# Background matmuls of an attention stream: one 128x128 matmul each in place of four 128x32 column tiles

## The chip, the cores and the metric

The kernel runs on one core of one Trainium2 chip. The metric is the device time of one execution in microseconds (us). Three runs of the kernel before took 1203.0, 1203.92 and 1205.25 us; the median is 1203.92 us.

## The reference

The computation is one transformer layer on 2048 tokens of width 1024, in bf16: layer norm, attention with 32 heads of width 32, a residual, a second layer norm, and a feed-forward block of width 3584 with tanh-GELU and another residual.

```python
x = A_x
h = x + _A_ref(_layernorm(x, axis=-1), A_wqkv, A_wo)      # softmax attention, 32 heads, then @ wo
h2 = h + _B_ref(_layernorm(h, axis=-1), B_w1, B_b1, B_w2, B_b2)   # gelu(x @ w1 + b1) @ w2 + b2
```

## The kernel before, in words

**Engines.** TensorE (PE) does all matrix products, ScalarE (ACT) does the softmax exponentials and the tanh of the GELU, VectorE (DVE) moves results out of PSUM and does the layer norms, SyncE (SP) issues the loads and stores. Each engine runs its own instruction stream in order, and semaphores tie the streams together.

**The attention stream.** The queries are cut into four chunks of 512. For each chunk and each of 16 pairs of heads, `attention_round` runs 8 times, so there are 512 rounds in all. A round issues three kinds of work.

- **qk** (`Att.qk`, L634): four matmuls with a contraction of 32 rows each. They sit in four *row* tiles of the array, at row 0, 32, 64 and 96, run side by side, and fill four PSUM banks with scores (keys on the partitions, 512 queries along the free dimension).
- **exp** (L643): two ACT instructions, each on two banks (128x1024), write the exponentials `PT` in bf16. Three pairs of banks go round, so one pair is free while two are in use.
- **pv** (`Att.pv_unit`, L654 and L658): for each exponential tile four matmuls with 32 output columns each, in four *column* tiles of the array: two heads of P times V, and two with a stationary block of ones that sum the softmax denominators. They accumulate in bank 6 over the 16 key tiles.

**The background stream.** Exponentials take long, so PE gets other work to fill the time: in the first chunk the rest of the Q, K and V projections (`proj`, `proj_v`), in the later chunks the output projection, the second layer norm and the feed-forward block of the chunk before (`wo`, `ln2`, `ffn1`, `ffn2`) and the late part of the query projection (`late_q`). It all goes through PSUM bank 7 (banks 4 and 7 in the opening). After the last attention chunk, the last chunk's `wo`, `ln2`, `ffn1` and `ffn2` run alone, with all eight banks; this is the tail.

**`mm`** issues one background product of 128 contraction rows, 128 output partitions and 512 (in `proj_v` 256) free elements. Its argument `narrow` is true in the background stream and false in the tail. With `narrow` it issues four matmuls (L439), each with 32 columns of `lhsT` as its stationary operand, at column tiles 0, 32, 64 and 96, all with the same moving operand. Without, it issues a single 128x128 matmul (L443). So in the kernel before the background and pv both use the array as four column tiles.

**What sets the order.** The kernel is first recorded as a graph of tasks, and `Graph.schedule` plays it through with estimated costs to fix the order of each engine's stream at build time. `pick_pe` takes a ready qk first, then a pv when four or five of them wait, else a background task. The task of one `mm` carries a cost `occ` and a `mode` ("col", "row" or "full"); a change of mode adds 0.1 us in this plan, and `pick_pe` looks at the mode "col" too. The plan decides the order alone; on the chip the streams run as fast as their semaphores let them. The planner's marks for a narrow `mm` are one task of mode "col".

**Transposes.** `transposes` (L508) are 128x128 matmuls in the background stream before and after the change; eight of them form one tile.

Of the kernel before, what the change touches and what calls it, by code (L numbers as in the profile page):

```python
# [284 lines left out]
def build_kernel(nc, A_x, A_wqkv, A_wo, B_w1, B_b1, B_w2, B_b2, out):  # L285
# [123 lines left out]
    psum = nc.alloc_psum_tensor("ps", [P, 8, 512], F32)  # L409
    B_ps = [gr.buf() for _ in range(8)]  # L410
# [18 lines left out]
    def pe(fns, occ, reads=(), writes=(), kind="bg", mode="full", prio=0, after=()):  # L429
        return gr.add(E.PE, fns, occ, 0.16, reads, writes, prio, kind, mode, after)  # L430

    def mm(bank, lhsT, rhs, start, stop, reads, narrow, cols=(0, 512)):

        c0, c1 = cols
        occ = MM * (c1 - c0) / 512.0 + 0.003
        if narrow:
            fns = []
            for j in range(4):
                fns.append(lambda p, j=j: p.matmul(psum[32 * j:32 * j + 32, bank, c0:c1], lhsT[:, 32 * j:32 * j + 32], rhs,  # L439
                                                   start=start, stop=stop, tile_position=(0, 32 * j), skip_group_check=True))  # L440
            pe(fns, occ, reads=reads, writes=[B_ps[bank]], mode="col")
        else:
            pe(lambda p: p.matmul(psum[:, bank, c0:c1], lhsT, rhs, start=start, stop=stop),  # L443
               occ, reads=reads, writes=[B_ps[bank]], mode="full")

    def act(fn, n, reads=(), writes=(), prio=0, ap_bias=False, kind=""):
        return gr.add(E.Activation, fn, c_act(n, ap_bias), 0.14, reads, writes, prio, kind)
# [7 lines left out]
    def dma(out_ap, in_ap, nbytes, reads=(), writes=(), prio=0, noncontig=False, after=()):  # L455
        def fn(s):
# [10 lines left out]
         reads=[B_ident], writes=[B_ident])  # L467
# [67 lines left out]
    def proj(which, g, tc, bank, evac, direct=False):  # L535

        blk, c = divmod(which * D + g * P, 512)
        for dc in range(DC):
            mm(bank, Wall[:, blk, dc, c:c + P], xnT[:, tc, dc, :], dc == 0, dc == DC - 1,
               [B_W[blk][c // P]] + B_xnTt[tc], True)  # L540
        s = cnt["sg"] % NSG
        cnt["sg"] += 1
        if evac == "act":
            act(lambda a: a.activation(stg[:, s, :], psum[:, bank, :], ACT.Copy), 512,
                reads=[B_ps[bank]], writes=[B_stg[s]], prio=-1)
        else:
            dve(lambda v: v.tensor_copy(stg[:, s, :], psum[:, bank, :]), c_dve_ps(512), reads=[B_ps[bank]], writes=[B_stg[s]])  # L547
        if which == 1:
            for pr in range(2):
                for half in range(2):  # L550
                    dve(lambda v, pr=pr, half=half: v.tensor_copy(
                        KT2[64 * half:64 * half + 64, 2 * g + pr, tc, :, :],
                        stg[64 * pr:64 * pr + 64, s, 256 * half:256 * half + 256]), c_dve(256, 4),
                        reads=[B_stg[s]], writes=[B_KT[4 * (2 * g + pr) + tc][half]])
        else:
            if direct:
                for pr in range(2):
                    for half in range(2):
                        dve(lambda v, pr=pr, half=half: v.tensor_copy(
                            QT2[64 * half:64 * half + 64, g, pr, :], stg[64 * pr:64 * pr + 64, s, :]), c_dve(512, 4),  # L560
                            reads=[B_stg[s]], writes=[B_QTh[g][half][pr]], prio=-1)
            else:
                dma(qd[g, tc], stg[:, s, :], P * 1024, reads=[B_stg[s]], writes=[B_qd[g][tc]], prio=0)
# [12 lines left out]
    def late_q(R, qc, gs):  # L576

        dma(R.xq[:, :, :], xd[qc - 1], P * 8192, reads=[B_xd[qc - 1]], writes=[R.B_xq], prio=0)
        for g2 in range(gs // 2, G // 2):
            s = wblock(R, A_wqkv[:, 256 * g2:256 * g2 + 256], 0)  # L580
            for k in range(2):
                g = 2 * g2 + k
                for dc in range(DC):
                    mm(7, R.w1[:, s, dc, k * P:k * P + P], R.xq[:, dc, :], dc == 0, dc == DC - 1,
                       [R.B_w1[s], R.B_xq], True)
                o = R.next("os", R.nos)
                dve(lambda v, o=o: v.tensor_copy(R.ost[:, o, :], psum[:, 7, :]), c_dve_ps(512),
                    reads=[B_ps[7]], writes=[R.B_ost[o]])
                dma(qd[g, qc], R.ost[:, o, :], P * 1024, reads=[R.B_ost[o]], writes=[B_qd[g][qc]], prio=0)

    def proj_v(tt, q, bank, evac):

        blk, c = divmod(256 * q, 512)
        blk += 4
        for k in range(2):
            tc, t4 = divmod(tt + k, 4)
            for dc in range(DC):
                mm(bank, xnT[:, tc, dc, t4 * P:(t4 + 1) * P], Wall[:, blk, dc, c:c + 256], dc == 0, dc == DC - 1,
                   B_W[blk][c // P:c // P + 2] + [B_xnTt[tc][t4]], True, cols=(256 * k, 256 * k + 256))
        dst = V[:, tt:tt + 2, 256 * q:256 * q + 256]  # L600
        src = psum[:, bank, :].rearrange("p (t c) -> p t c", t=2)
        wr = [B_V[4 * (tt + k) + q] for k in range(2)]
        if evac == "act":
            act(lambda a: a.activation(dst, src, ACT.Copy), 512, reads=[B_ps[bank]], writes=wr, prio=-1)
        else:
            dve(lambda v: v.tensor_copy(dst, src), c_dve_ps(512), reads=[B_ps[bank]], writes=wr)  # L606
# [190 lines left out]
    for k in range(80):  # L797
        pe(lambda p: p.matmul(psum[:, 6, 0:256], ident[:, :], b2t[:, 0:256], start=True, stop=True), 0.12,  # L798
           reads=[B_ident, B_b2t], writes=[B_ps[6]], kind="warm")
# [207 lines left out]
```

## Time and profile before

| what | value |
|---|---|
| median of three runs | 1203.92 us (1203.0 to 1205.25) |
| span of the profiled execution | 1417.9 us |
| mean granted TensorE clock in it | 0.749 of full speed |
| PE busy | 1366.2 us, 96% of the span, 17326 matmuls |
| ACT busy | 1085.3 us, 77% |
| DVE busy | 673.2 us, 47% |
| last exponential starts | 1253.9 us after the span's start |

The profile shows a single execution, and the profiler gives no other time for it than its span, 1417.9 us, from the first instruction to the last. That is 214 us above the median of the three timed runs, which carry no profile. A matmul's end is modelled in these records, and its start is observed, so in what follows matmuls are judged by the distance from one start to the next. A *group* is what one call issues together: four tiles that start within some 12 ns of each other, or one full matmul. The granted clock is what a throttle lets through to TensorE.

### The profile page before, as it was taken

To read this page: it belongs to the slowest core of one execution; us is meant where nothing else is said; L and a number is where in the kernel's file an instruction comes from. 1 tells how busy PE (TensorE), PEld (TensorE's weight loads), DVE (VectorE), ACT (ScalarE), POOL (GpSimd) and SP (SyncE) were. 2 spreads that over 40 slices of the span, in tenths; PEclk is the share of its full clock that TensorE was granted. 3 is DMA by queue.
4 is the path that set the end of the run, shared out by engine and by line. 5 is a ranking of instruction groups with operands and counts; after the bars stand their busy time and mean duration, and the time that the engine had idled before them with its cause. 6 is when DMAs were issued, how large, how long until landed. Compare 5 with 4: busy or idle time off the path is not lost.

```text
span 1417.9 us, 37847 instructions
## 1 busy us (share of the span) xinstructions
PE 1366.2 (96%) x17326; PEld 510.9 (36%) x17336; DVE 673.2 (47%) x1165; ACT 1085.3 (77%) x1189; POOL 37.9 (3%) x96
## 2 busy tenths in 40 slices
PE   8999999999999999999999999999999999978999
PEld 5544443433333333332333333333333333324333
DVE  7354444443546774223547762225677612245710
ACT  4778787878888888888888888888988888844500
POOL 2000000000100000000100000000000000001000
PEclk7777777777777777777777777777777777766777
DMA  6800000025343222303342230422323322202222
GB/s 165 224 2 13 28 13 14 13 72 156 101 122 101 76 69 72 124 16 98 107 124 71 83 98 16 124 71 63 107 73 98 102 66 85 87 0 75 74 93 71
DMA packets 165793, 112.29 MB, mean 79 GB/s; under 512 B 25345, under 2 KB 162817, under 8 KB 164866
## 3 DMA queue, kind: packets, MB, share of 16 engines
q1 hardware_dynamic: 165634, 109.87, 26.2%
q8 instruction: 136, 2.23, 0.7%
q14 instruction: 23, 0.19, 0.1%
HBM read 98.58 MB, written 11.27 MB: 77 GB/s over the span
## 4 chain that ended last, share of the span: by engine, by line
PE 91%; ACT 4%; DVE 3%; issue 1%; POOL 1%; DMA 0%; POOLq 0%; DVEq 0%
PE ps L439 48%; PE ps L654 17%; PE ps L634 12%; PE ps L443 10%; ACT PT L643 3%; PE ps L658 2%; PE ps L798 1%; ACT xnT L512 1%; DVE a_xh L748 1%; PE ps L508 1%; DVE V L606 0%; DVE stg L547 0%; DVE Osb L668 0%; DVE Dsb L666 0%; DMA a_w1r<-in_A_wqkv_dram 0%
## 5 line engine op out<-in xcount | busy, mean ns | idle before, releaser
L643 ACT ACTIVATE PT<-ps 128x1024 bf16<-128x1024 f32 x1024 | 989.2, 1025 | 180.5 <-PE ps L634 166.1
L654 PE MATMUL ps<-PT,V 128*32 128x512 bf16 x2048 | 383.4, 457 | 13.7 <-DVE V L606 6.2
L658 PE MATMUL ps<-PT,ones 128*32 128x512 bf16 x2048 | 384.8, 458 | 0.0
L439 PE MATMUL ps<-a_w2r,gT 128*32 128x512 bf16 x2688 | 241.9, 452 | 0.0
L634 PE MATMUL ps<-QT,KT 32*128 32x512 bf16 x2048 | 216.7, 414 | 7.4 <-ACT PT L643 7.3
L439 PE MATMUL ps<-a_hnT,a_w1r 128*32 128x512 bf16 x2688 | 215.2, 454 | 4.0 <-DVE a_xh L748 3.2
L654 PEld LDWEIGHTS ps<-PT,V 128*32 128x32 bf16 x2048 | 103.3, 104 | 143.9 <-issue 89.3
L634 PEld LDWEIGHTS ps<-QT,KT 32*128 32x128 bf16 x2048 | 51.5, 91 | 272.3 <-ACT PT L643 164.5
L439 PE MATMUL ps<-xnT,Wall 128*32 128x512 bf16 x1344 | 111.6, 453 | 7.0 <-ACT xnT L512 4.8
L439 PEld LDWEIGHTS ps<-a_w2r,gT 128*32 128x32 bf16 x2688 | 77.3, 109 | 112.0 <-issue 103.3
L673 DVE RECIPROCAL Dsb<-Dsb 128x128 f32<-128x128 f32 x128 | 115.1, 928 | 1.0
L439 PEld LDWEIGHTS ps<-a_hnT,a_w1r 128*32 128x32 bf16 x2688 | 70.6, 107 | 108.0 <-issue 71.4
L782 DVE SCALAR_TENSOR_TENSOR a_ost<-ps,hch 128x512 bf16<-128x512 f32 x24 | 16.6, 692 | 189.8 <-PE ps L439 189.7
L658 PEld LDWEIGHTS ps<-PT,ones 128*32 128x32 bf16 x2048 | 103.5, 104 | 6.6 <-issue 6.6
L748 DVE TENSOR_SCALAR a_xh<-ps,b1f 128x512 bf16<-128x512 f32 x84 | 63.1, 751 | 81.3 <-PE ps L439 80.2
L666 DVE COPY Dsb<-ps 64x512 f32<-64x512 f32 x64 | 44.4, 694 | 101.5 <-PE ps L658 100.1
L439 PE MATMUL ps<-Wall,xnT 128*32 128x256 bf16 x2048 | 83.8, 314 | 0.0
L547 DVE CAST stg<-ps 128x512 bf16<-128x512 f32 x40 | 27.5, 689 | 89.2 <-PE ps L439 89.2
L443 PE MATMUL ps<-a_hnT,b_w1r 128*128 128x512 bf16 x219 | 64.5, 470 | 2.1 <-ACT a_hnT L512 1.5
L439 PEld LDWEIGHTS ps<-Wall,xnT 128*32 128x32 bf16 x2048 | 57.6, 107 | 22.7 <-issue 11.3
L443 PE MATMUL ps<-a_w2r,gT 128*128 128x512 bf16 x219 | 64.1, 461 | 0.5
L439 PE MATMUL ps<-a_w1r,OT 128*32 128x512 bf16 x768 | 63.1, 453 | 0.8 <-DVE hch L719 0.5
(69 smaller groups left out, 875.5 us busy)
## 6 DMA issues: line engine op xcount, KB each, us to landing
a_w2r<-in_B_w_dram SPq DMA_DIRECT2D x56, 512.0 KB, 4.6
a_w1r<-in_B_w_dram SPq DMA_DIRECT2D x42, 512.0 KB, 3.9
a_w1r<-in_A_wo_dram SPq DMA_DIRECT2D x16, 512.0 KB, 4.7
QT<-q_scratch SPq DMA_DIRECT2D x60, 128.0 KB, 2.8
b_w1r<-in_B_w_dram SPq DMA_DIRECT2D x14, 512.0 KB, 3.8
a_w1r<-in_A_wqkv_dram SPq DMA_DIRECT2D x11, 512.0 KB, 5.1
xrb<-in_A_x_dram SPq DMA_DIRECT2D x16, 256.0 KB, 3.9
Wall<-in_A_wqkv_dram SPq DMA_DIRECT2D x16, 256.0 KB, 5.4
```

The source lines that it names most:

```text
L439: fns.append(lambda p, j=j: p.matmul(psum[32 * j:32 * j + 32, bank, c0:c1], lhsT[:, 32 * j:32 * j + 32], rhs, start=start, stop=stop, tile ...
L443: pe(lambda p: p.matmul(psum[:, bank, c0:c1], lhsT, rhs, start=start, stop=stop), occ, reads=reads, writes=[B_ps[bank]], mode="full")
L508: pe(lambda p, dc=dc: p.transpose(psb[:, bank, dc * P:(dc + 1) * P], src_ap[:, dc * P:(dc + 1) * P], ident[:]), 0.064, reads=[B_src, B_ide ...
L547: dve(lambda v: v.tensor_copy(stg[:, s, :], psum[:, bank, :]), c_dve_ps(512), reads=[B_ps[bank]], writes=[B_stg[s]])
L634: return p.matmul(psum[:, 2 * u + j, :], KT2[r0:r0 + 32, p16, tc, i, :], QT2[r0:r0 + 32, qs, pr, :], start=True, stop=True, tile_position= ...
L643: act(lambda a, u=u, s=s: a.activation(PT[:, s, :, :], psum[:, 2 * u:2 * u + 2, :], ACT.Exp, bias=0.0, scale=SCALE), 1024, reads=[B_ps[2 * ...
L654: fns.append(lambda p, j=j, h=h: p.matmul(psum[32 * j:32 * j + 32, bank, :], V[:, kt, 32 * h:32 * h + 32], PT[:, s, j, :], start=first, st ...
L658: fns.append(lambda p, j=j: p.matmul(psum[64 + 32 * j:96 + 32 * j, bank, :], ones32[:, :], PT[:, s, j, :], start=first, stop=last, tile_po ...
L666: dve(lambda v: v.tensor_copy(Dsb[64 * pr:64 * pr + 64, :], psum[64:128, bank, :]), c_dve_ps(512), reads=[B_ps[bank]], writes=B_Dsb[pr], p ...
L673: dve(lambda v, k=k: v.reciprocal(Dsb[:, 128 * k:128 * k + 128], Dsb[:, 128 * k:128 * k + 128]), 0.93, reads=[B_Dsb[0][k], B_Dsb[1][k]], w ...
L748: dve(lambda v, i=i, fc=fc, bank=bank: v.tensor_scalar(R.xh[:, i, :], psum[:, bank, :], b1f[:, fc:fc + 1], None, ALU.add), c_dve_ps(512), ...
L782: dve(lambda v, o=o, t4=t4, j=j, bank=bank: v.scalar_tensor_tensor(R.ost[:, o, :], psum[:, bank, :], 0.5, hch[:, t4, 512 * j:512 * j + 512 ...
```

## The change

`mm` issues one 128x128 matmul in every case. Its stationary operand is the whole 128x128 `lhsT`, the moving operand and the PSUM region stay as they were. The planner's marks are kept: the task still has the same cost and, for `narrow`, the mode "col".

```diff
         occ = MM * (c1 - c0) / 512.0 + 0.003
-        if narrow:
-            fns = []
-            for j in range(4):
-                fns.append(lambda p, j=j: p.matmul(psum[32 * j:32 * j + 32, bank, c0:c1], lhsT[:, 32 * j:32 * j + 32], rhs,
-                                                   start=start, stop=stop, tile_position=(0, 32 * j), skip_group_check=True))
-            pe(fns, occ, reads=reads, writes=[B_ps[bank]], mode="col")
-        else:
-            pe(lambda p: p.matmul(psum[:, bank, c0:c1], lhsT, rhs, start=start, stop=stop),
-               occ, reads=reads, writes=[B_ps[bank]], mode="full")
+        pe(lambda p: p.matmul(psum[:, bank, c0:c1], lhsT, rhs, start=start, stop=stop),
+           occ, reads=reads, writes=[B_ps[bank]], mode="col" if narrow else "full")
```

The built programs have the same order on every engine; on PE each four instructions of L439 become one. 10336 column-tile matmuls become 2584 full ones (2072 with 512 free elements, 512 with 256). Matmuls of the tail, qk, pv and the transposes are untouched.

## Prediction

> **What bounds the kernel now.** I read the page from the top: busy shares, the clock by slices, the chain that ended last.
>
> ```profile
> span 1417.9 us, 37847 instructions
> ...
> PE 1366.2 (96%) x17326; PEld 510.9 (36%) x17336; DVE 673.2 (47%) x1165; ACT 1085.3 (77%) x1189; POOL 37.9 (3%) x96
> ...
> PEclk7777777777777777777777777777777777766777
> ...
> PE 91%; ACT 4%; DVE 3%; issue 1%; POOL 1%; DMA 0%; POOLq 0%; DVEq 0%
> ```
>
> PE is busy nearly throughout, holds 91% of the chain, and gets a clock of 0.75. So the profiled execution is bound by PE. The groups show who could be next:
>
> ```profile
> L643 ACT ACTIVATE PT<-ps 128x1024 bf16<-128x1024 f32 x1024 | 989.2, 1025 | 180.5 <-PE ps L634 166.1
> ...
> L634 PE MATMUL ps<-QT,KT 32*128 32x512 bf16 x2048 | 216.7, 414 | 7.4 <-ACT PT L643 7.3
> ```
>
> ACT's exponentials wait 166 us for qk; qk waits 7 us for them. Wherever PE is longer, ACT is later.
>
> The timed runs are 214 us shorter, so their balance must be worked out. The program has 4384 groups of 512 columns (2072 + 256 background, counting two of 256 as one; 512 qk, 1024 pv, 520 tail) and some 104 equivalents in warm-up and transposes. In the tail's run of full matmuls the starts lie 292 ns apart at clock 0.752 (504 pairs), in column-tile runs 277 ns (2544 pairs); at full clock that is about 216 ns. 4488 x 0.216 = 969 us of pure streaming, or 1289 us at 0.752. The runs take 1204, so their clock is higher: at least 969/1204 = 0.80, and with 1069 mode changes at some 0.08 us and 40 us of opening and tail waits about 0.90. ACT's floor in the attention part is 992 exponentials at 0.912 us (starts back to back lie 0.904 to 0.920 apart) plus 84 tanh at 0.52 = 948 us; PE's there, at full clock, is 969 - 49 (the opening: 152 groups and 72 equivalents) - 114 (the tail: 520 and 8) + 90 (changes of mode) = 896. So between clock 0.90 and 1.0 PE and ACT are within 6% of each other, and PE has at most 52 us to spare.
>
> **What the change does.** The order of the streams stays. *Removed:* three of four instructions of each background group. That pays only if the group is held by something other than its 512 columns. The 256-column groups answer this: with the same eight instructions (four weight loads, four matmuls) they follow each other in 138 ns on average (430 pairs), which is 256 columns at 0.75. So issue keeps up at 17 ns an instruction, and a 512 group would need no more than 138 of its 277. I book no gain. Weight loads are hidden in both shapes:
>
> ```profile
> L439 PEld LDWEIGHTS ps<-a_hnT,a_w1r 128*32 128x32 bf16 x2688 | 70.6, 107 | 108.0 <-issue 71.4 <-DVE a_xh L748 23.9
> ...
> L443 PEld LDWEIGHTS ps<-a_hnT,b_w1r 128*128 128x128 bf16 x224 | 25.6, 115 | 40.6 <-issue 39.2 <-ACT a_hnT L512 1.4
> ```
>
> 107 and 115 ns lie inside a pitch of 277 to 292. The Trainium skill (TensorE: Matmul & The Clock Gate, Weight-path perf modes) says a full 128-column bf16 weight gets a fast load, and TensorEngine Tiling (Array Packing), Restrictions, that column tiling disables it: a rule in favour of the change. The two rows differ by 8 ns the other way; with a hidden load the sum by the rule stays the same.
>
> *Added:* changes of the array's division. Before, background and pv are both column tiles and follow each other at the common pitch; only qk (row tiles) stands between:
>
> ```profile
> 468.22 0.40 PE L634 MATMUL ps<-QT,KT 32*128 32x512 bf16 x4
> 468.63 2.10 PE L439 MATMUL ps<-a_hnT,a_w1r 128*32 128x512 bf16 x28
> 470.66 0.42 PE L634 MATMUL ps<-QT,KT 32*128 32x512 bf16 x4
> 471.02 0.45 PE L439 MATMUL ps<-a_hnT,a_w1r 128*32 128x512 bf16 x4
> 471.24 0.48 PE L654 MATMUL ps<-PT,V 128*32 128x512 bf16 x2
> ```
>
> Columns: start, length, engine, line, operation. Row to column costs 0.41 and 0.36 us instead of one pitch; background to pv costs 0.22, nothing extra. Over the trace: column to row 406 ns (449 pairs), row to column 354 (491). After the change each border of background and pv is a border of full and column. In the built order the changes of mode go from 1069 to 1813: 372 pairs (full to column and back) are new, and some 370 qk neighbours turn from column to full. The trace of before has this very sequence near the end, where the tail's `wo` begins inside the last rounds:
>
> ```profile
> 1234.45 0.43 PE L654 MATMUL ps<-PT,V 128*32 128x512 bf16 x2
> 1234.46 0.49 PE L658 MATMUL ps<-PT,ones 128*32 128x512 bf16 x2
> 1234.88 0.97 PE L443 MATMUL ps<-a_w1r,OT 128*128 128x512 bf16 x3
> 1235.78 0.45 PE L634 MATMUL ps<-QT,KT 32*128 32x512 bf16 x4
> 1236.16 1.24 PE L443 MATMUL ps<-a_w1r,OT 128*128 128x512 bf16 x4
> 1237.33 0.41 PE L654 MATMUL ps<-PT,V 128*32 128x512 bf16 x2
> ```
>
> pv to full took 0.43 here; the trace has 426, 385, 382 and one 579 that held a wait, mean of the three 398 ns. Full to pv took 360, 380, 360, mean 367. From transposes to pv it is 171 against 70 between transposes (17 and 226 pairs), again +100.
>
> - **Term 1, new changes.** Against a pitch of 284 (between 277 and 292): (398 - 284) + (367 - 284) = 197 ns a pair, x 372 = 73 us. Bounds: 158 ns (fastest of each, against 292) gives 59; 256 ns (579 kept in, against 277) gives 95.
> - **Term 2, qk beside full.** qk to full 379 (one) and to transposes 367 (6) against 354; full to qk 415 (one) against 406. 370 x (13 + 3 to 9), about 6 us; bounds 0 and 12.
> - **Term 3, catching up.** In column runs the first pitch after a change is 248 ns (476 runs), 32 below the 280 or so of the later ones: part of the stop is regained. 744 more runs, x 32 = -24 us. This may belong to the throttle, whose pitches jump between 266 and 318; and a run of a single group has no second pitch. Bounds -24 and 0; I take -24.
> - **Term 4, pitch in runs.** 277 against 292 is the same first-pitch effect, since column runs are short and the tail's long; taken as 0. No bound beyond Term 3.
>
> Sum: 73 + 6 - 24 = 55 us on PE, between 59 + 0 - 24 = 35 and 95 + 12 = 107. In the profile's own time nothing covers this, as PE is the chain: 1418 + 55 = **1473 us**. In the timed runs the clock is 0.90 or more; a stop counted in cycles shrinks to 0.8 of itself (58 of the 73), but so does the regained part, and a stop made of latencies keeps its size. I keep 55: 1204 + 55 = **1259 us**.
>
> The skill has the rule against this change (TensorEngine Tiling, Tiling Modes, Key Properties): a change of tiling mode drains TensorE, while another tile of one mode does not. It names no price; TensorE: Matmul & The Clock Gate gives a drain of about 128 cycles, an estimate of 53 ns at 2.4 GHz and 40 us for 744, against 55 by the rows.
>
> No DMA, wait or buffer is added. pv and qk come later by the stops in front of them; waiting on them are the exponentials on ACT, then the next qk.
>
> **The rivals.**
>
> - *ACT covers it.* If the timed clock is 1.0, PE has 52 us to spare in the attention part and the 55 are mostly hidden: about 1204 + 8 = 1212. For it: 948 against 896. Against: the timed attention part is then 1204 - 75 (opening, 82 less half of the 16 that the clock can give) - 124 (tail, 161 less 37 for the clock) = 1005, 57 above ACT's floor, so ACT would already be waiting for PE; and the plan fills each round of PE with background.
> - *The stops cost their upper bound* and nothing is regained: 1204 + 107 = 1311. For it: at a higher clock the throttle's catching up may go. Against: three of four samples.
> - *Faster.* At the timed clock the four-tile group may be held by issue. The most this can be is the excess of 1005 over PE's 896, 109 us over some 2200 background groups, 50 ns each. Taking it away and adding 55 leaves PE at 951 and the time at about 1150. It decides from 25 ns a group (55/2200). Against: 138 ns for eight instructions.
> - *Nothing happens:* the array passes from full to column tiles without a stop: 1204. Against: every sample.
>
> **Numbers.** Forecast 1259 (within 1230 to 1295): 0.64. Hidden by ACT, 1205 to 1230: 0.16. Upper bound, 1295 to 1320: 0.11. Faster, 1150: 0.06. Nothing, 1204: 0.03. A measurement of this kernel tells apart about 0.2%, 2.4 us. Faster 0.06; same 0.03 and 0.01 of the hidden case: 0.04; slower 0.90. The range leaves out faster, nothing and the upper bound: 1210 to 1300.
>
> **What would show it.** In the profile after: PE matmuls 17326 less some 7750; pv to background near 398 and background to pv near 367 where they were at the common pitch; runs of background unchanged at 280 to 290; ACT's wait for qk up from 166 by about 55; DVE and the tail unchanged. If pv to background stays at 280, Term 1 is wrong. If the stops show in the profile but the timed runs stay near 1210, ACT covered them. If background runs are shorter in pitch than before, issue did matter.

## Result and the profile after

| | before | after |
|---|---|---|
| median | 1203.93 us (1203.0 to 1205.25, 4 runs) | 1255.85 us (1255.47 to 1256.85, 4 runs) |
| ratio to before | | 1.0433, 95% interval 1.0418 to 1.0448 |

The change costs 51.9 us, or 4.3%. The forecast was 1259 us, within 1210 to 1300.

The profiled execution on which the prediction rests had a granted clock of 0.75 and took 1417.9 us, while all later ones had 0.99 and took what the timed runs take, so from here on before is read in a second profile of the same kernel (experiment e1, span 1200.8 us). Its page, in the rows that were shown above (the last one is the chain of work that ended last, by engine):

```profile
span 1200.8 us, 37847 instructions
...
PE 1126.8 (94%) x17326; PEld 465.6 (39%) x17336; DVE 668.4 (56%) x1165; ACT 1059.5 (88%) x1189; POOL 38.1 (3%) x96
...
PE 74%; ACT 12%; DVE 10%; DMA 2%; issue 1%; POOL 1%; SPq 0%; POOLq 0%; DVEq 0%
```

The same rows of after:

```profile
span 1253.7 us, 22353 instructions
...
PE 1192.3 (95%) x9584; PEld 421.2 (34%) x9584; DVE 670.9 (54%) x1165; ACT 1073.1 (86%) x1189; POOL 37.9 (3%) x96
...
PE 82%; DVE 8%; ACT 7%; issue 1%; DMA 1%; POOL 1%; POOLq 0%; DVEq 0%; SPq 0%
```

The records of PE hold 7742 matmuls fewer (the built programs differ by 7752), and PE is busy 65 us longer. It holds 82% of the chain in place of 74%. Where the time goes is seen in one place of the second chunk's `ffn2`, the same instructions in both. The timeline of before (e1), PE alone (columns: start, length, engine, line, operation):

```profile
505.53 0.40 PE L634 MATMUL ps<-QT,KT 32*128 32x512 bf16 x4
505.85 0.40 PE L439 MATMUL ps<-a_w2r,gT 128*32 128x512 bf16 x4
506.08 0.38 PE L654 MATMUL ps<-PT,V 128*32 128x512 bf16 x2
506.08 0.38 PE L658 MATMUL ps<-PT,ones 128*32 128x512 bf16 x2
506.29 0.39 PE L439 MATMUL ps<-a_w2r,gT 128*32 128x512 bf16 x4
506.51 0.38 PE L654 MATMUL ps<-PT,V 128*32 128x512 bf16 x2
506.52 0.38 PE L658 MATMUL ps<-PT,ones 128*32 128x512 bf16 x2
506.73 0.82 PE L439 MATMUL ps<-a_w2r,gT 128*32 128x512 bf16 x12
507.48 0.40 PE L634 MATMUL ps<-QT,KT 32*128 32x512 bf16 x4
```

And of after:

```profile
520.54 0.40 PE L627 MATMUL ps<-QT,KT 32*128 32x512 bf16 x4
520.86 0.39 PE L436 MATMUL ps<-a_w2r,gT 128*128 128x512 bf16 x1
521.18 0.39 PE L647 MATMUL ps<-PT,V 128*32 128x512 bf16 x2
521.19 0.39 PE L651 MATMUL ps<-PT,ones 128*32 128x512 bf16 x2
521.52 0.39 PE L436 MATMUL ps<-a_w2r,gT 128*128 128x512 bf16 x1
521.84 0.39 PE L647 MATMUL ps<-PT,V 128*32 128x512 bf16 x2
521.84 0.39 PE L651 MATMUL ps<-PT,ones 128*32 128x512 bf16 x2
522.17 0.82 PE L436 MATMUL ps<-a_w2r,gT 128*128 128x512 bf16 x3
522.92 0.39 PE L627 MATMUL ps<-QT,KT 32*128 32x512 bf16 x4
```

From one qk to the next it is 1.95 us before and 2.38 after. Background to pv and pv to background take 0.22 us before and 0.32 to 0.34 after, four times in this round: 4 x 0.107 = 0.43 us. Nothing else in the round is different.

The weight loads (PEld) show what is different at such a border. In a stretch of after there are two background products, a border, and two pv:

```profile
450.36 0.61 PE L436 MATMUL ps<-a_hnT,a_w1r 128*128 128x512 bf16 x2
450.89 0.10 PEld L647 LDWEIGHTS ps<-PT,V 128*32 128x32 bf16 x2 [0.42 <-issue]
450.89 0.39 PE L647 MATMUL ps<-PT,V 128*32 128x512 bf16 x2
...
450.91 0.10 PEld L647 LDWEIGHTS ps<-PT,V 128*32 128x32 bf16 x2
...
451.12 0.38 PE L647 MATMUL ps<-PT,V 128*32 128x512 bf16 x2
```

The second pv's weights are loaded 0.21 us ahead of its matmul, beside the first pv; the first pv's weights are loaded only as its own matmul starts. Over the trace of after the load's lead is 214 ns (median) between background groups and 213 between pv, and 2 to 4 ns at every border of pv, background and qk; in e1 it is 214 between pv and background too, and 2 to 4 at the borders of qk. So at a border nothing of the next group runs ahead. Whether the stop is PE running out of the group before, or the load that has not run ahead, these records do not separate, and no run tried it.

Distances from start to start over the whole trace, 512-column groups, median ns (mean of those under 600 in brackets):

| from, to | before (e1) | after |
|---|---|---|
| background to background | 216 (219) | 216 (220) |
| background to pv | 216 (222) | 319 (316) |
| pv to background | 216 (248) | 332 (344) |
| background to qk | 322 (324) | 312 (312) |
| qk to background | 325 (330) | 327 (332) |

**The ledger.** For the part from the first exponential to the last (1048.2 us in e1, 1099.5 after) I took every distance less 216 ns for 512 columns, counted up to 110 ns at each change of the array's division as a stop, and the rest as a wait. Stops: 114.0 before, 188.5 after, +74.5 us. Waits: 93.5 before, 70.9 after, -22.6. The sum is +51.9; the part grew by 51.3 and the tail by 2.1. The largest wait is pv to background, 37.4 us before and 20.4 after. The profile names who ends a wait; the idle time of PE in e1 (a part of these waits, as a matmul's modelled length runs into them), by who ended it:

```profile
PE ps L634 <- ACT PT L643: 13.1, 31, 1.1
PE ps L439 <- DVE a_xh L748: 11.3, 35, 1.0
...
PE ps L439 <- DVE stg L547: 3.3, 9, 0.6
PE ps L439 <- DVE a_ost L782: 3.2, 7, 0.7
```

and after:

```profile
PE ps L627 <- ACT PT L636: 11.4, 26, 1.1
...
PE ps L436 <- DVE a_xh L741: 6.5, 19, 0.8
...
PE ps L436 <- DVE a_ost L775: 2.2, 5, 0.5
PE ps L436 <- DVE stg L540: 1.8, 6, 0.5
```

Columns: total us, times, longest. The DVE rows are the instructions that empty bank 7, the background's only accumulator. A background product waits there until VectorE has emptied the bank: in e1 33 of the 37 us end within 150 ns (55 or some 147) after one of these instructions. A stop ahead of the product makes it later, and so the wait shorter. The rows of ACT, where qk waits for exponentials, hardly differ.

### The profile page after: what moved, and what is told of

It is laid out like the page before. It is cut to its first block, busy times and chain, and to the rows that moved or that the text cites. A ratio compares the mean times of both kernels' runs of the same rounds, so it can differ in the third digit from the quotient of the medians.

```text
span 1253.7 us, 22353 instructions
## 1 busy us (share of the span) xinstructions
PE 1192.3 (95%) x9584; PEld 421.2 (34%) x9584; DVE 670.9 (54%) x1165; ACT 1073.1 (86%) x1189; POOL 37.9 (3%) x96
## 3 DMA queue, kind: packets, MB, share of 16 engines
q1 hardware_dynamic: 165634, 109.87, 29.9%
## 4 chain that ended last, share of the span: by engine, by line
PE 82%; DVE 8%; ACT 7%; issue 1%; DMA 1%; POOL 1%; POOLq 0%; DVEq 0%; SPq 0%
PE ps L436 52%; PE ps L647 16%; PE ps L627 11%; ACT PT L636 6%; DVE a_xh L741 3%; ACT xnT L505 1%; PE ps L791 1%; DVE a_uu L749 1%; DVE Dsb L666 1%; DVE gT L753 1%; DVE V L599 1%; DVE Dsb L659 0%; DVE Osb L661 0%; DVE stg L540 0%; ACT a_th L751 0%
## 5 line engine op out<-in xcount | busy, mean ns | idle before, releaser
L636 ACT ACTIVATE PT<-ps 128x1024 bf16<-128x1024 f32 x1024 | 980.4, 1028 | 70.1 <-PE ps L627 49.2
L647 PE MATMUL ps<-PT,V 128*32 128x512 bf16 x2048 | 320.9, 386 | 13.8 <-DVE V L599 5.4
L651 PE MATMUL ps<-PT,ones 128*32 128x512 bf16 x2048 | 320.9, 386 | 0.0
L436 PE MATMUL ps<-a_w2r,gT 128*128 128x512 bf16 x896 | 248.0, 382 | 0.1
L627 PE MATMUL ps<-QT,KT 32*128 32x512 bf16 x2048 | 202.7, 386 | 11.9 <-ACT PT L636 11.4
L436 PE MATMUL ps<-a_hnT,a_w1r 128*128 128x512 bf16 x672 | 172.8, 381 | 7.7 <-DVE a_xh L741 6.0
L436 PEld LDWEIGHTS ps<-a_w2r,gT 128*128 128x128 bf16 x896 | 75.8, 97 | 129.9 <-issue 76.3
L436 PE MATMUL ps<-xnT,Wall 128*128 128x512 bf16 x336 | 90.5, 382 | 7.6 <-ACT xnT L505 5.4
L436 PE MATMUL ps<-Wall,xnT 128*128 128x256 bf16 x512 | 67.9, 274 | 0.0
L436 PE MATMUL ps<-a_w1r,OT 128*128 128x512 bf16 x256 | 66.1, 383 | 1.5 <-DVE hch L712 0.6
L540 DVE CAST stg<-ps 128x512 bf16<-128x512 f32 x40 | 27.4, 685 | 68.9 <-PE ps L436 68.8
L753 DVE SCALAR_TENSOR_TENSOR gT<-a_th,a_xh 128x512 bf16<-128x512 f32 x84 | 56.8, 677 | 3.3 <-ACT a_th L751 2.8
L749 DVE SCALAR_TENSOR_TENSOR a_uu<-a_sq,a_xh 128x512 bf16<-128x512 bf16 x84 | 56.7, 678 | 1.4
```

What stands on the lines that cost most here:

```text
L627: return p.matmul(psum[:, 2 * u + j, :], KT2[r0:r0 + 32, p16, tc, i, :], QT2[r0:r0 + 32, qs, pr, :], start=True, stop=True, tile_position= ...
L636: act(lambda a, u=u, s=s: a.activation(PT[:, s, :, :], psum[:, 2 * u:2 * u + 2, :], ACT.Exp, bias=0.0, scale=SCALE), 1024, reads=[B_ps[2 * ...
L647: fns.append(lambda p, j=j, h=h: p.matmul(psum[32 * j:32 * j + 32, bank, :], V[:, kt, 32 * h:32 * h + 32], PT[:, s, j, :], start=first, st ...
L651: fns.append(lambda p, j=j: p.matmul(psum[64 + 32 * j:96 + 32 * j, bank, :], ones32[:, :], PT[:, s, j, :], start=first, stop=last, tile_po ...
L749: dve(lambda v, i=i: v.scalar_tensor_tensor(R.uu[:, i, :], R.sq[:, i, :], C2, R.xh[:, i, :], ALU.add, ALU.mult), c_dve(512), reads=[R.B_sq ...
L753: dve(lambda v, i=i, fc=fc: v.scalar_tensor_tensor(gT[:, fc, :], R.th[:, i, :], 1.0, R.xh[:, i, :], ALU.add, ALU.mult), c_dve(512), reads= ...
```

## Experiments

Theory S: each change of the array's division stops PE for about 0.11 us, and part of it is covered by something, which the first expectations take to be ACT. Rivals: the full matmul itself costs more (F); the price of an added change is a flat 52/744 = 0.07 us (P); ACT is what covers (first rival of the prediction); issue held the column tiles (I).

**e1: the kernel before again.** No edit.

> The kernel before, unchanged, for a profile at the clock of the timed runs. If the granted clock is about 0.99, the span should be near 1203 us, runs of column tiles should follow at 216 ns, background and pv should follow each other at 216 too, and column to row and back should take about 315 and 330 ns. Theory S (each change of the array's division stops PE for some 0.11 us, in part covered by ACT) expects PE to have tens of us to spare here; the rival I (a column-tile group is held by issue at full clock) expects a pitch of 240 ns or more.

1202.56 us (one run). Clock 0.993, background pitch 216: I falls. The column-to-row and row-to-column distances are 322 and 325 ns. Whether PE has "tens of us to spare" beside ACT this profile alone does not settle: e5 tests it.

**e2: pv as a full matmul too**, in the kernel after.

```diff
-            fns = []
-            for j in range(2):
-                h = 2 * p16 + j
...
+            v0 = 128 * (p16 // 2)
+            fns = [lambda p: p.matmul(psum[:, bank, :], V[:, kt, v0:v0 + 128], PT[:, s, 0, :], start=first, stop=last)]
```

> The kernel after, with pv too as one 128x128 matmul; it leaves out half of the attention product and the softmax denominators (one head's exponentials times 128 columns of V), with the same 512 columns streamed, the same order, reads and waits. Changes of the array's division: 1024, against 1813 after and 1069 before. Theory S: the whole loss goes, 1204 us or a few us less. Rival F (a full matmul in the background costs some 20 ns more than a group of column tiles, whatever stands beside it): stays at 1256 or higher, as more groups are full.

1196.0 us, ratio to before 0.994 (0.9922 to 0.9958). Background to pv and back are at 216 ns again. The background's 2584 full matmuls are all still there, so F falls: a full matmul costs nothing beside another full one. The loss belongs to the border of full and column tiles.

**e3: two column tiles of 64**, in the kernel before.

```diff
-            for j in range(4):
-                fns.append(lambda p, j=j: p.matmul(psum[32 * j:32 * j + 32, bank, c0:c1], lhsT[:, 32 * j:32 * j + 32], rhs,
-                                                   start=start, stop=stop, tile_position=(0, 32 * j), skip_group_check=True))
+            for j in range(2):
+                fns.append(lambda p, j=j: p.matmul(psum[64 * j:64 * j + 64, bank, c0:c1], lhsT[:, 64 * j:64 * j + 64], rhs,
+                                                   start=start, stop=stop, tile_position=(0, 64 * j), skip_group_check=True))
```

> The kernel before, with each background group as two column tiles of 128x64 in place of four of 128x32. Same order; no full matmul in the background. Divisions differ between 64 and 32 columns: 1819 changes. Theory S, if a stop comes with any change of tile size: about 1256 us. If only full against tiled stops: about 1204. Rival F expects about 1204 to 1230.

1267.67 us, ratio 1.0534 (1.0509 to 1.0558): slower than after. The timeline of e3 shows a tiled background stopping beside a tiled pv:

```profile
526.33 0.41 PE L439 MATMUL ps<-a_w2r,gT 128*64 128x512 bf16 x2
526.66 0.39 PE L654 MATMUL ps<-PT,V 128*32 128x512 bf16 x2
526.67 0.39 PE L658 MATMUL ps<-PT,ones 128*32 128x512 bf16 x2
526.99 0.41 PE L439 MATMUL ps<-a_w2r,gT 128*64 128x512 bf16 x2
```

0.33 and 0.32 us. It is not full against tiled that matters but one tile size against another. Over the trace background to pv is 336 ns here and 319 after. Why 17 more, and where the rest of the 12 us between e3 and after comes from, was not tried.

**e4: the change in `ffn2` alone.** The two `mm` calls of `ffn2` issue a full matmul; the planner's mark stays "col".

```diff
...
-                       [B_gT[fc], R.B_w2[s]], len(banks) == 1)
+                       [B_gT[fc], R.B_w2[s]], False, as_col=len(banks) == 1)
```

> The change in ffn2 alone (696 of 2584 groups); the planner's marks and the order are those of before. 1415 changes, 346 more than before and 46% of the added 744. Theory S: 46% of the 52 us, 1228 us (less if the stage has more cover than the others). Rival F: 696 of 2584 groups, 27%, 1218 us.

1239.16 us, ratio 1.0299 (1.028 to 1.0317): 35.5 us for 346 changes, 103 ns each, and 68% of the whole loss for 46% of the changes. Both S with even cover (1228) and F (1218) are too low. The cover is uneven: this stage has almost none.

**e7: the change in `ffn1` alone**, in the same way.

> The change in ffn1 alone (672 of 2584 groups). 1226 changes, 157 more than before, 21% of the added 744. Theory S with the cover where the traces place it (in the ffn1 stages ACT has the tanh as well, and there after lost only some 2 us a chunk): 1206 to 1211. Rival P (the same price for each change everywhere): 1215. Rival F: 26% of the groups, 1217.

1209.14 us, ratio 1.0041 (1.0026 to 1.0056): 5.3 us for 157 changes, 34 ns each. P and F fall. The number is the one that S expected, but S had put the cover down to ACT. Between the same exponentials, number 320 to 416 (mostly `ffn1`), e1 takes 106.6 us and after 108.6; from 416 to 512 (`ffn2`) it is 90.4 and 101.6. The stage table of e1 shows the two stages' engines:

```profile
core 0: us, PE busy (x) PEld busy (x) DVE busy (x) ACT busy (x) POOL busy (x), PEclk, DMA share, GB/s
362.00:468.00 106.00, 99.81 (x1572) 37.07 (x1568) 88.02 (x142) 103.95 (x124) 0.00 (x0) 1.00 0.35 101
468.00:559.00 91.00, 89.61 (x1456) 33.89 (x1452) 25.88 (x35) 90.46 (x98) 0.00 (x0) 1.00 0.30 90
```

In `ffn1` VectorE is busy for 88 of 106 us and empties bank 7 every eight groups; in `ffn2` for 26 of 91, and the bank is emptied every 29. The ledger by stage, e1 against after and so in one order, says the same (each distance is counted to the stage of the next background product). In `ffn2`, which runs three times in the background, stops grow by 35.1 us (32.5 to 67.6), waits go from 7.2 to 6.8, and the stage takes 34.9 us more. In `ffn1` stops grow by 15.0 (27.4 to 42.4), waits fall by 10.7 (29.9 to 19.2), 9.3 of it from pv to background, and the stage takes 4.3 more.

But ACT is nearly full in both. The next pair takes ACT away.

**e5 and e6: half of each exponential left out**, before and after.

```diff
-                act(lambda a, u=u, s=s: a.activation(PT[:, s, :, :], psum[:, 2 * u:2 * u + 2, :], ACT.Exp, bias=0.0, scale=SCALE),
+                act(lambda a, u=u, s=s: a.activation(PT[:, s, 0, :], psum[:, 2 * u, :], ACT.Exp, bias=0.0, scale=SCALE),
...
```

> The kernel before with half of each exponential left out (512 of 1024 elements; both heads of a pair then use the first head's exponentials). Order, PE work and waits are the same; ACT's floor in the attention part falls from some 948 to some 560 us, so ACT covers nothing any more. Theory S: PE's own time shows, 806 streaming + about 1000 changes x 0.11 = 916 us between an opening and a tail as before, in all some 1110 to 1140.

1189.21 us, ratio 0.9875 (0.9859 to 0.9892).

> The kernel after with the same half of the exponentials left out. Theory S: with the cover gone all 744 added changes show at about 0.11 us, 80 to 95 us above e5. Rival P (each added change costs 0.07 us, and nothing is covered): 52 above e5, as with whole exponentials.

1241.18 us, ratio to before 1.0313 (1.0297 to 1.0328), 52.0 above e5. Both expectations of S, as I had it, miss: before gains only 15 us when ACT loses 400 us of work (1059.5 to 658.9 us busy), and the difference stays 52. The waits of ACT for qk, in e1:

```profile
ACT PT L643 <- PE ps L634: 18.9, 40, 2.5
```

and in e5:

```profile
ACT PT L643 <- PE ps L634: 358.5, 422, 3.8
```
So ACT was full but was not the bound: freed, it waits for PE. The kernel before is bound mostly by PE and by PE's waits for bank 7; ACT costs it some 15 us, and of the added stops it covers nothing. What is left is theory B: a stop costs PE 0.11 us, and the background's wait for bank 7 takes part of it back. By itself the difference of 52 is also what P expected, so one more pair had to take the bank's wait away.

**e10 and e11: two banks for the background**, on e5 and e6.

```diff
-    att.n_units = 3
+    att.n_units = 2
...
+    def bgb():
+        nbg[0] += 1
+        return (7, 4)[nbg[0] % 2]
...
-                bank = banks[nb % len(banks)]
+                bank = bgb() if len(banks) == 1 else banks[nb % len(banks)]
```

> e5 (half of each exponential left out) with two banks in turn for the background, 7 and 4, so that it seldom waits for VectorE to empty bank 7; the scores use two pairs of banks in place of three, and the planner knows the shorter exponentials. The order is a new one. Theory S: with the waits of pv to background (some 37 us) mostly gone, 1130 to 1175; the two pairs of banks may make qk wait and take some of it back.

1125.39 us, ratio to before 0.9349 (0.9335 to 0.9364). The waits from pv to background fell to 2.9 us, all waits to 21.0.

> e10 with one full matmul for each background group; the same order as e10, in which pv and background alternate more: 2664 changes against 1060, 1604 more. Theory B (a stop costs PE 0.11 us; what took back 23 of 75 us was the background's wait for bank 7, not ACT): nearly all of 1604 x 0.11 = 176 us above e10, at least 155. Rival P (0.07 us for each added change, whatever waits): 112 above e10. Rival A (ACT covers): as P or less is not expected, since ACT has half its work.

1294.77 us, ratio to before 1.0752 (1.0737 to 1.0767): 169.4 above e10, 106 ns for each of 1604 added changes. The stop is 0.106 us where nothing takes it back. Theory B holds, and P falls. (The pair differs from e5 and e6 in its order too, since the planner knows both the banks and the shorter exponentials, and the scores have two pairs of banks in place of three; between e10 and e11 the order is the same.)

**e8: the planner is told "full"**, in the kernel after.

```diff
-           occ, reads=reads, writes=[B_ps[bank]], mode="col" if narrow else "full")
+           occ, reads=reads, writes=[B_ps[bank]], mode="full")
```

> The kernel after with the planner told the truth: the background's task has mode full, so that each change between pv and background costs 0.1 us in the plan and pv is kept together where it can be. The order changes: 1693 changes in place of 1813. Theory S: 120 fewer, each worth 0.07 to 0.11 us where not covered, 1243 to 1250. Rival (the loss comes from something else than the changes): 1256.

1219.06 us, ratio to before 1.0125 (1.011 to 1.0141). Both expectations miss. It gains 37 us over after, of which 120 stops are only 13. So most of the gain comes with the order.

**e9: the order of e8 with column tiles.**

> The order of e8 (planner marks the background full) with the background of the kernel before, four column tiles a group. 1066 changes, against 1693 in e8. Theory S: 627 fewer stops of 0.11 us are 69 us on PE, less what waits take back: 1160 to 1180. If e8 gained over the kernel after because its order moves some 43 us of background behind the last exponential, where it costs only 17, this also beats the kernel before. Rival (e8's 1219 is set by its order, and not by the stops left in it): 1205 to 1219.

1207.16 us, ratio 1.0025 (1.0015 to 1.0036). The expectation of S misses by 27 us or more, and the rival's range, 1205 to 1219, holds: 627 stops fewer bring 11.9 us, 19 ns each, where 627 x 0.106 would be 66. In this order waits take back most of what the stops cost. In e9's ledger stops are at 114.4, as before, but waits at 101.0: pv to background 41.6 and background to qk 18.2, against 37.4 and 3.4 in e1. This can be read so that an order made for an array that stops leaves PE with nothing to do where it does not stop; it was not tested further. And the 94 background groups (20 us) that this order leaves behind the last exponential lengthen the tail by 16 us, so they fill little of a gap there.

**e12: exponentials at their measured cost in the plan**, in the kernel before.

```diff
-        return 0.100 + (0.093 if ap_bias else 0.0) + n / 1200.0
+        return 0.059 + (0.093 if ap_bias else 0.0) + n / 1200.0
```

> The kernel before with the planner's cost of an ACT instruction lowered by 0.041 us, so that an exponential costs 0.912 us in the plan, as measured, in place of 0.953. Less background fits beside the planned exponentials, and more is left for the time after them. 1065 changes. If the gain of e8's order is background that fills PE's wait at the start of the tail, this gains too: 1185 to 1200. If not, 1204 within 3.

1190.25 us, ratio 0.9884 (0.9871 to 0.9898): faster than both kernels by 13.7 and 65.6 us. The reason in its expectation is not the right one: 75 groups (16 us) go behind the last exponential, and the tail grows by 12 (128.6 to 140.8), so only 4 us are gained there. Waits in the attention part fall from 93.5 to 84.4. Together that is the size of the gain; which of the new order's steps shortens the waits stays open.

## Why the prediction was right, and where it was not

- **Direction and mechanism: right.** The streams keep their order, each border of pv and background becomes a stop, and the 744 added changes make the loss. e2 removes the borders and the loss, and e3 makes a loss of 64 us without a full matmul in the background.
- **What is removed brings nothing: right.** Background to background is 216 ns in both kernels, and inside a run the weight loads, 96 ns for 128x32 and 97 for 128x128, stay hidden. At a border neither shape is loaded ahead; the prediction read the loads by their length alone and did not see that.
- **Term 1: 197 ns a pair expected, about 219 measured** (319 and 332 against 216): 81 us in place of 73. The six samples from the end of the trace of before, three each way, were good enough.
- **Term 2: 6 us expected, about -3 measured.** qk to background is 2 ns longer, background to qk 10 ns shorter.
- **Term 3, catching up: wrong.** At clock 0.99 the first pitch of a background run after a change is 226 ns on average in after (450 runs) and in e1, and pv to pv has a median of 226 in after, not less than 216. Nothing is regained in that way. The shorter first pitch shows only in the profile at clock 0.75; the prediction itself said that it may belong to the throttle, and still took the 24 us off in full.
- **What covers: wrong engine.** "ACT covers it" was weighed as a rival, and the timed attention part was read as ACT and PE within 6%. (Its price, 1204 + 8, does not follow from its numbers, 55 less 52.) e5 and e6 show that ACT covers nothing of the stops; its wait for qk grew by 30 us (18.9 to 49.2), where 55 was expected. Of the 23 us in 75 that were taken back, 17 are the background's wait for bank 7 (pv to background), 9 of them in `ffn1`, where VectorE is busy. The rows for it stood in the first profile (PE ps L439 waits for DVE a_xh, stg, a_ost), small, and I did not price them.
- **The sum is closer than its terms.** 73 + 6 - 24 = 55 was forecast; 74.5 - 22.6 = 51.9 was found. An error of 24 and an omission of 23 met, so it is luck that 1259 lies within 3 us of 1255.85; without it the terms as measured, 81 and -3, would have given 1282.
- **The clock of the timed runs: right in its bound**, 0.90 or more; it was 0.99. The floor of PE at full clock, 896 us, lacked the waits for bank 7 and had 90 us of stops where the ledger has 114.

## What to carry to other kernels

Where two streams of small products share the array in turn, give them the same tile size: the border cost 0.106 us, half of a 512-column product, for full against 32 columns and about the same for 64 against 32, and the number of borders in the built order times this price is the first estimate, from above. What showed in the time here went from 19 ns a border (e8 against e9) over 34 (`ffn1`), 70 (the whole change) and 103 (`ffn2`) to 106 (e10 against e11). Then ask which wait stands directly behind the stop on the same engine, stage by stage: a short accumulator chain with one bank hid two thirds of the stops in `ffn1`, a long one hid nothing in `ffn2`. That another engine looks full does not make it the cover; halve its work and see.

## What was not expected of the hardware

- A stop is not a fixed count of cycles of the granted clock: column to row and back cost 406 + 354 - 2 x 277 = 206 ns a pair by the means of the profile at clock 0.75 (415 + 351 - 2 x 266 = 234 by the medians), which would be 156 (177) ns at 0.99, and there it is 322 + 325 - 2 x 216 = 215.
- Two column tile sizes stop each other as full and column tiles do (pv to background and back: 329 and 336 ns in e3, 332 and 319 after).
- At a change of the array's division the next group's weights are not loaded ahead: the load starts 2 to 4 ns before its matmul, and 213 or 214 ns before it inside a run (medians of after).
